# Adding the upsampled rows inside the local products, with P divided before its transposes

## Chip, cores and metric

One core of a Trainium2 chip runs the whole kernel. The metric is device time in microseconds of one execution; a kernel's time is the median over its runs. A profile of one execution gives the trace from which the rows below are taken. Engines: PE multiplies matrices, DVE and ScalarE (ACT) work on elements and read PE's results, GpSimd (POOL) works on elements in SBUF, SyncE (SP) issues most of the DMAs.

## The reference

Attention over 8 batches, 8 heads, 576 positions, 64 dimensions, in two branches that are added, and then a mixture of 8 experts. All is float32. Cut to what is computed:

```python
# coarse branch: means over 4 positions, full attention over 144, every row used for 4 positions
q_d = q.reshape(B, H, Sd, 4, D).mean(axis=3)           # k_d, v_d alike
out_up = np.repeat(softmax_attention(q_d, k_d, v_d), 4, axis=2)
# local branch: only |i - j| < 4
scores = np.where(mask, scale * q @ k.T, -1e9)
attn = np.exp(scores - max)
attn = attn / (np.sum(attn, axis=-1, keepdims=True) + 1e-09)
x = out_up + attn @ v                                  # then to (4608, 512)
# experts: logits x @ w_gate; pairs (token, expert) in falling order of logit, 576 tokens
# for each expert; out[tokens of e] = relu(x @ w1[e]) @ w2[e]
```

## The kernel before

The program has three stages: the attention with the logits, the routing, and the experts. Instructions of the attention stand on each engine exactly in the order in which the code is called; that order comes from tables of numbers.

**Local branch.** It goes in 36 units of 128 tokens. A unit u has four windows of 32 queries; the 38 keys that a window can reach lie in a block `KW`. For each unit, in units of time after u (the table `LOC`):

- `s0`, `s1` (0.33): scores of four heads each on PE, over a mask that is added by a matmul; then on DVE a maximum (`mx`, line 444) and a subtraction into the tile `sw` (line 445). ScalarE takes the exponential in place three PE pieces later (`FL`, line 446).
- `t` (1.3): four transposes of `sw` on PE (line 454), copied by ScalarE into `pt` (line 465), so that keys lie on partitions.
- `v0`, `v1` (1.83): products of `pt` with the values, 32 matmuls of 65 columns (line 476). The values are in one of four tiles `vw`, two windows to a tile half: window c takes partitions from 64 (c mod 2) on. 48 rows are loaded for a window (`VR`) of which 38 are used; rows 48 to 63 of each half have nothing. A 65th column of ones makes PE sum P, and `norm` (lines 404, 405, 407) divides by that sum on DVE while it moves the products from PSUM into `x`.
- `up` (1.7, but not before the coarse branch of the batch is through): a DMA of the upsampled rows from `up_dram` to the tile `up`, 32 rows of 2 KB, each four times, 256 KB (line 416).
- `add` (4.5): x + up (line 484), on DVE, from unit 28 on POOL. `st` (4.6): x to DRAM (line 487).
- `lt` (5.61): transposes of x (line 494), split in two halves of 16 bits by ScalarE (line 498) and DVE (line 499). `lm` (8.07): logits (lines 509, 512, 514).

**Coarse branch.** For each batch (4.5 units) q and k are transposed (`trw`, `trt`; `TW` says from when to when, counted from the batch before), summed over 4 positions (`gsum`, mostly on POOL), and then `down` runs six pieces of scores and transposes and two of products (`DW`, counted from the batch's first unit). Its last step divides on DVE, writes to `up_dram` (lines 387, 394), and `load_up` reads it back. `evac` sends the copies of transposes out of PSUM to DVE or ScalarE in turn, by the tuple `EV`: a 1 is DVE.

`run` gives every step a time, sorts them, and calls them; a PE step counts as a piece, and `after(n, f)` calls f n pieces later. `need(key)` calls it at once. All loads and stores of the attention are issued by SP in that order. `load_vw(u)` stands 1.75 units before unit u (`VWT`). The profile's lines are those of the code here:

## Time and profile before

| | us |
|---|---|
| median of 3 runs (781.58 to 786.01) | 782.59 |
| the profiled execution | 783.71 |
| its span, first to last instruction | 781.8 |
| busy in the span: PE / DVE / ACT / POOL | 681.8 / 560.7 / 332.0 / 244.0 |
| last logits of the attention reduced | 291.3 |

A row of a busy-time view gives a stretch and how long each engine worked in it. A row of waits names who waited, what ended the wait, and the total. A row of groups gives the line in the code, engine, operation, what it writes and reads, then count, busy time and mean duration, and idle time of the engine ahead of it. Idle time of an engine costs only where somebody waits for that engine.

### The profile page before, as it was taken

How to read it: one execution, taken by the hardware profiler on the slowest of the kernel's cores; microseconds unless marked ns; L12 is line 12 of the kernel's file. 1: busy time of each engine (PE TensorE's matmuls, PEld its weight loads, DVE VectorE, ACT ScalarE, POOL GpSimd, SP SyncE). 2: the span in 40 equal slices, each digit the busy share in tenths (PEclk: the TensorE clock that was granted, in tenths of full speed). 3: DMA queues.
4: the chain of work that ended last, by engine and by line, in shares of the span. 5: the costliest groups of instructions: out<-in, count | busy, mean ns of one | idle time of the engine just before them, and what ended most of it. 6: DMA issues, size and time to landing. Idle time of an engine off the chain costs nothing.

```text
span 781.8 us, 21171 instructions
## 1 busy us (share of the span) xinstructions
PE 681.8 (87%) x8565; PEld 470.8 (60%) x8565; DVE 560.7 (72%) x1679; ACT 332.0 (42%) x631; POOL 244.0 (31%) x274
## 2 busy tenths in 40 slices
PE   6788889888888863499899999999989999999994
PEld 4676778777767652365465465366457476574752
DVE  7978888778868887787969979798959645171210
ACT  3546758465576440441524425134225234262210
POOL 9455364535626340300710512121230402201001
PEclk9889999989999995599899999999999999999998
DMA  9959899897988650712615565562743783804001
GB/s 265 208 163 266 213 228 258 231 245 236 239 224 197 173 175 1 238 40 87 217 35 191 153 154 178 102 240 60 228 169 105 124 278 76 215 2 101 22 27 34
DMA packets 148133, 125.00 MB, mean 160 GB/s; under 512 B 92228, under 2 KB 122436, under 8 KB 148036
## 3 DMA queue, kind: packets, MB, share of 16 engines
q1 hardware_dynamic: 140656, 102.12, 48.6%
q0 software_dynamic: 6432, 20.98, 8.9%
q8 instruction: 68, 1.11, 0.6%
q10 hardware_dynamic: 948, 0.55, 0.3%
q14 instruction: 29, 0.24, 0.1%
HBM read 95.30 MB, written 21.23 MB: 149 GB/s over the span
## 4 chain that ended last, share of the span: by engine, by line
PE 30%; issue 25%; DVE 24%; DMA 10%; POOL 4%; ACT 4%; SPq 1%; POOLq 0%; ACTq 0%; DVEq 0%
PE pX L1135 7%; PE pH L1106 7%; POOL out_dram L1144 2%; DVE cmp L703 2%; PE pR L733 2%; DMA up<-up_dram 2%; DMA nat<-in_moe_w_dram 2%; PE g L476 2%; DVE x L407 2%; PE g L292 1%; DMA vw<-in_v_dram 1%; PE g L373 1%; DVE x L484 1%; DVE wl L1054 1%; PE g L436 1%
## 5 line engine op out<-in xcount | busy, mean ns | idle before, releaser
L1106 PE MATMUL pH<-xt,wh 128*128 128x256 f16 (+1 forms) x1024 | 196.9, 287 | 2.8 <-DMA xt<-xs 1.1
L1135 PE MATMUL pX<-wh,ht 128*128 128x512 f16 (+1 forms) x640 | 183.3, 386 | 1.9 <-DVE xt L1082 1.9
L1106 PE MATMUL pH<-xt,wl 128*128 128x320 f16 (+1 forms) x512 | 146.3, 287 | 0.0
L1135 PEld LDWEIGHTS <-ht 128*128 128x128 f16 (+1 forms) x960 | 82.5, 101 | 90.6 <-issue 7.0
L1144 POOL DMA_INDIRECT out_dram<-y,idx x40 | 44.3, 1109 | 285.2 <-ACT y L1141 226.4
L1135 PE MATMUL pX<-wl,ht 128*128 128x512 f16 (+1 forms) x320 | 119.9, 387 | 0.0
L1106 PEld LDWEIGHTS <-wh 128*128 128x128 f16 x1024 | 97.6, 98 | 29.0 <-issue 3.5
L1119 ACT ACTIVATE ht<-pH 128x512 f16<-128x512 f32 (+1 forms) x128 | 45.5, 407 | 124.1 <-PE pH L1106 124.1
L1054 DVE SCALAR_TENSOR_TENSOR wl<-nat,wh 128x512 f16<-128x512 f32 x128 | 84.8, 684 | 2.9 <-ACT wh L1052 0.7
L1069 POOL DMA_INDIRECT xg<-x_dram,idx x40 | 49.2, 1231 | 106.9 <-DVE idx L1004 36.0
L1141 ACT ACTIVATE y<-pX 128x512 f32<-128x512 f32 (+1 forms) x40 | 23.7, 593 | 131.8 <-PE pX L1135 75.9
L1122 DVE SCALAR_TENSOR_TENSOR ht<-pH,ht 128x512 f16<-128x512 f32 (+1 forms) x128 | 52.6, 452 | 34.6 <-ACT ht L1119 34.1
L1052 ACT ACTIVATE wh<-nat 128x1024 f16<-128x1024 f32 x64 | 66.8, 1055 | 10.4 <-DMA nat<-in_moe_w_dram 10.3
L1106 PEld LDWEIGHTS <-wl 128*128 128x128 f16 x512 | 50.1, 98 | 11.9
L465 ACT COPY pt<-g 64x512 f32<-64x512 f32 x72 | 41.7, 580 | 28.8 <-PE g L454 26.3
L476 PE MATMUL g<-vw,pt 128*64 128x65 f32 x1152 | 44.6, 231 | 6.7 <-ACT pt L465 4.6
L1143 DVE SCALAR_TENSOR_TENSOR y<-pX,y 64x512 f32<-64x512 f32 x8 | 5.5, 694 | 61.7 <-ACT y L1141 61.6
L476 PEld LDWEIGHTS g<-vw,pt 128*64 128x64 f32 x1152 | 39.6, 144 | 12.9 <-ACT pt L465 7.5
L292 PE MATMUL g<-ident,nat 128*128 128x128 f32 x256 | 41.9, 292 | 4.4 <-DMA nat<-in_k_dram 3.2
L265 POOL TENSOR_TENSOR gtmp<-qz 64x576 f32<-64x576 f32 x28 | 32.0, 1144 | 32.9 <-DVE kdt L268 31.2
L278 ACT COPY kt<-g 64x512 f32<-64x512 f32 (+1 forms) x56 | 35.2, 628 | 16.7 <-PE g L292 10.5
L484 DVE TENSOR_TENSOR x<-x,up 128x512 f32<-128x512 f32 x28 | 29.6, 1058 | 15.0 <-DMA up<-up_dram 15.0
(219 smaller groups left out, 1197.8 us busy)
## 6 DMA issues: line engine op xcount, KB each, us to landing
nat<-in_moe_w_dram SPq DMA_DIRECT2D x28, 1024.0 KB
vw<-in_v_dram SPq DMA_DIRECT2D x136, 96.0 KB
up<-up_dram SPq DMA_DIRECT2D x36, 256.0 KB
x_dram<-x SPq DMA_DIRECT2D x36, 256.0 KB
nat<-in_q_dram SPq DMA_DIRECT2D x16, 512.0 KB
nat<-in_k_dram SPq DMA_DIRECT2D x16, 512.0 KB
nat<-in_v_dram SPq DMA_DIRECT2D x14, 512.0 KB
up_dram<-xu SPq DMA_DIRECT2D x16, 128.0 KB
```

The lines of the kernel that those rows point to most:

```text
L292: nc.tensor.transpose(p[:, a, :, fp], src[:, 4 * hh + 2 * a + s, 2 * fp:2 * fp + 2].rearrange("p f d -> p (f d)"), self.ident)
L465: self.nc.scalar.copy(out, in_)
L476: nc.tensor.matmul(o[64 * i:64 * i + 64, 65 * h:65 * h + 65], pt[:, 2 * g + i, h].rearrange("p b q -> p (b q)"), self.vw[u % 4][:, i, 4 * ...
L484: (nc.gpsimd if u >= ADDU else nc.vector).tensor_tensor(x, x, self.up[u], op=OP.add)
L1052: nc.scalar.activation(hi, r, AF.Copy, scale=sc)
L1054: nc.vector.scalar_tensor_tensor(lo[:, a:a + LOP], r[:, a:a + LOP], sc, hi[:, a:a + LOP], op0=OP.mult, op1=OP.subtract)
L1069: self.fetched = nc.gpsimd.indirect_dma_start(out=xg[:n], out_offset=None, in_=self.x, in_offset=bass.IndirectOffsetOnAxis(ap=idx[:n, c:c ...
L1106: mm = nc.tensor.matmul(p[:, s, :s1 - s0], w[d][a][:, 128 * f:128 * f + 128], xt[:, b, d, s0:s1], start=j == 0, stop=j == len(seq) - 1)
L1119: last = nc.scalar.activation(hi, q, AF.Relu)
L1122: nc.vector.scalar_tensor_tensor(lo, q, 0.0, hi, op0=OP.max, op1=OP.subtract)
L1135: mm = nc.tensor.matmul(p[o:o + m], ht[:, f, h0:h0 + m], w[4 + f // 2][b][:, 512 * (f % 2):512 * (f % 2) + 512], start=j < parts, stop=j > ...
L1144: i = nc.gpsimd.indirect_dma_start(out=self.out, in_=y[:n], in_offset=None, out_offset=bass.IndirectOffsetOnAxis(ap=idx[:n, c:c + 1], axis=0))
```

## The change

P is divided by its sum right after the exponential, on DVE (`norm` in `loc_s`), so the column of ones goes, and ScalarE copies the products into x as they are. The upsampled rows of a unit (8 for each window, 32 in all) are loaded into partitions 48 to 55 and 112 to 119 of the unit's `vw` tile, two DMAs of 32 KB. Columns 48 to 55 of `sw` hold fixed ones, which give each query its row; the transposes carry them into `pt`, and so the products add the upsampled row. The adds are gone for all units but the first three (`OLD`), which keep the way of before. The write to `up_dram` is issued `FU` pieces after the coarse division. The coarse branch stands earlier, every second evacuation goes to DVE, there are three `sw` tiles instead of two, and the later steps of a unit have new times.

```diff
-DW = (0.15, 1.9)
-DWS = {0: (1.96, 3.4), 7: (0.82, 2.25)}
-LOC = {'up': 1.7, 'st': 4.6, 't': 1.3, 'lm': 8.07, 's0': 0.33, 's1': 0.331, 'lt': 5.61, 'v0': 1.83, 'v1': 1.831, 'add': 4.5}
+FM = 2
+FX = 1
+FU = 3
+TW = (0.16, 1.95)
+DW = ((-1.95, -0.05), (-1.4, 0.45))
+DWS = {0: (1.96, 3.4), 1: (-0.8, 0.7)}
+UPL = 0.4
+LOC = {'up': 1.2, 'st': 3.3, 't': 1.87, 'lm': 5.2, 's0': 0.33, 's1': 0.331, 'lt': 3.7, 'v0': 2.35, 'v1': 2.351}
+OLD = 3
-NSW = 2
+NSW = 3
-EV = (0,0,0,1)
+EV = (0,1)
-VWT = 1.75
+VWT = 1.6
...
             for t in self.sw:
                 nc.gpsimd.memset(t[:, :, KW:], 0.0)
+            for t in self.sw:
+                nc.gpsimd.tensor_copy(t[:, :, VR:VR + 8], self.spare[:, None].to_broadcast([128, H, 8]))
...
         def end():
             r = self.norm(o, x[:, :4], 4 + g, 4.0)
...
+            self.after(FU, put, ("u", b, g))
+
+        def put():
+            up = self.up_dram[b * G:b * G + 128, 256 * g:256 * g + 256]
+            nc.sync.dma_start(up, x[:, :4].rearrange("p h d -> p (h d)"))
...
         for b in {4 * u // NW, (4 * u + 3) // NW}:
             for g in range(2):
                 self.need(("v", b, g))
+                self.need(("u", b, g))
+        src = self.up_dram[32 * u:32 * u + 32]
+        if u >= OLD:
+            for i in range(2):
+                p0 = 64 * i + VR
+                self.nc.sync.dma_start(self.vw[u % 4][p0:p0 + 8].rearrange("p c h d -> p c (h d)"),
+                                       bass.AP(tensor=src.tensor, offset=src.offset + 8 * i * HD,
+                                               ap=[[HD, 8], [16 * HD, 2], [1, HD]]))
+            return
...
-        self.after(FL, lambda: nc.scalar.activation(t[:, :, :KW], t[:, :, :KW], AF.Exp, scale=0.125), ("l", u))
+        t = t[:, :, :KW]
+        self.after(FL, lambda: nc.scalar.activation(t, t, AF.Exp, scale=0.125), ("e", u))
+
+        def norm():
+            self.need(("e", u))
+            r = self.wk.tile([128, H], F32, name="dl", bufs=3)
+            nc.vector.tensor_reduce(r, t, axis=AX.X, op=OP.add)
+            nc.vector.tensor_scalar(r, r, 1e-9, None, op0=OP.add)
+            nc.vector.reciprocal(r, r)
+            nc.vector.tensor_tensor(t, t, r[:, :, None].to_broadcast([128, H, KW]), op=OP.mult)
+
+        self.after(FL + FM, norm, ("l", u))
...
-        self.norm(o, x[:, 256 * g:256 * g + 256].rearrange("p (h d) -> p h d", h=4), 4, 1.0)
+        if g:
+            x = self.x[u] = self.wk.tile([128, HD], F32, name="x", bufs=XB)
+            self.after(FX, lambda: nc.scalar.copy(x, o), ("o", u))
```

**How the order moves.** First DVE, at unit 24, from its maximum on (names: `den` is the reciprocal of the column of ones, `dl` that of the new sum, `xt` the halves of the transposed x, `lg` the logits, `sd` the coarse scores). Before:

```order
L444 TENSOR_REDUCE mx<-g 128x8
L445 TENSOR_TENSOR sw_131<-g,mx 128x8x38
L484 TENSOR_TENSOR x<-x,up 128x512
L499 SCALAR_TENSOR_TENSOR xt<-g,xt 128x512
L404 TENSOR_SCALAR den<-g 128x4
L405 RECIPROCAL den<-den 128x4
L407 TENSOR_TENSOR x<-g,den 128x256
L404 TENSOR_SCALAR den<-g 128x4
L405 RECIPROCAL den<-den 128x4
L407 TENSOR_TENSOR x<-g,den 128x256
L514 TENSOR_REDUCE lg<-g 128x8
```

And now, from the same maximum:

```order
L464 TENSOR_REDUCE mx<-g 128x8
L465 TENSOR_TENSOR sw_131<-g,mx 128x8x38
L472 TENSOR_REDUCE dl<-sw_131 128x8
L473 TENSOR_SCALAR dl<-dl 128x8
L474 RECIPROCAL dl<-dl 128x8
L475 TENSOR_TENSOR sw_131<-sw_131,dl 128x8x38
L534 SCALAR_TENSOR_TENSOR xt<-g,xt 128x512
L338 TENSOR_REDUCE mxd<-g 128x3
L340 TENSOR_TENSOR sd<-g,mxd 128x432
L549 TENSOR_REDUCE lg<-g 128x8
```

The add and two divisions of products out of PSUM are gone, and one division of P stands right behind the subtraction, ahead of the halves of x.

Second SP, where batch 4's coarse result goes out (`up_dram<-xu`) and the first unit that uses it, 18, reads it back. Before:

```order
L387 DMA up_dram<-xu 128x256
L487 DMA x_dram<-x 128x512
L200 DMA natt<-in_q_dram 64x1x256 x2
L200 DMA natt<-in_k_dram 64x1x256 x2
L387 DMA up_dram<-xu 128x256
L394 DMA up_dram<-xu 8x16x64
L416 DMA up<-up_dram 128x1x512
L229 DMA vw_129<-in_v_dram 48x8x64
```

And now, where unit 17's rows are loaded between the two writes:

```order
L404 DMA up_dram<-xu 128x256
L431 DMA vw_128<-up_dram 8x2x512 x2
L521 DMA x_dram<-x 128x512
L404 DMA up_dram<-xu 128x256
L406 DMA up_dram<-xu 8x16x64
L236 DMA vw_127<-in_v_dram 48x8x64 x4
L431 DMA vw_129<-up_dram 8x2x512 x2
```

The load stood right behind the write; now a unit's values stand between them, and the rows go into a `vw` tile.

Third PE, at the transposes of P (`sw`): unit 20's before, ahead of the scores of unit 21 (`kt,qz`), the logit transposes (`ident,x`) and unit 20's products (`vw,pt`):

```order
L454 MATMUL g<-ident,sw_131 128x128 x4
L428 LDWEIGHTS identb
L428 MATMUL g<-mask,identb 128x304
L436 MATMUL g<-kt,qz_119 32x38 x32
L494 MATMUL g<-ident,x 128x128 x4
L476 MATMUL g<-vw_127,pt_133 64x65 x16
```

And unit 19's now:

```order
L448 LDWEIGHTS identb
L448 MATMUL g<-mask,identb 128x304
L456 MATMUL g<-kt,qz_119 32x38 x32
L506 MATMUL g<-vw_129,pt_134 64x64 x16
L332 MATMUL g<-kdt,qdz_124 128x144 x3
L529 MATMUL g<-ident,x 128x128 x4
L332 MATMUL g<-kdt,qdz_124 128x144 x3
L485 MATMUL g<-ident,sw_132 128x128 x4
L332 MATMUL g<-kdt,qdz_124 128x144 x2
L335 MATMUL g<-kdt,qdt_125 32x144 x4
```

The transposes stood ahead of the next unit's scores; now they stand behind them, behind the products of unit 18 and pieces of batch 5's coarse scores (`kdt,qdz`).

More of the change, by code (lines that the diff above doesn't have):

```diff
@@ L106, in __init__ @@
         self.ident, ident = ident
-        identh = cst.tile([128, 130 + H], BF, name="identb")
-        self.identb, self.half, self.own8 = identh[:, :128], identh[:, 128:130], identh[:, 130:]
+        identh = cst.tile([128, 138 + H], BF, name="identb")
+        self.identb, self.half, self.own8 = identh[:, :128], identh[:, 128:130], identh[:, 130:130 + H]
+        self.spare = identh[:, 130 + H:]
         self.wm = cst.tile([128, 128], BF, name="wm")
@@ L126, in __init__ @@
         for i in range(4):
-            self.vw.append(cst.tile([128, 2, H, D + 1], F32, name=f"vw{i}"))
+            self.vw.append(cst.tile([128, 2, H, D], F32, name=f"vw{i}"))
         for i in range(NSW):
@@ L469, in loc_v @@
         if g == 0:
[L470 to L472 removed]
+            self.ov = self.ps.tile([128, 512], F32, name="g", bufs=8)
+        o = self.ov
         pt = self.ptw[u % NPT]
@@ L483, in log_a @@
         x = self.x[u]
-        (nc.gpsimd if u >= ADDU else nc.vector).tensor_tensor(x, x, self.up[u], op=OP.add)
+        self.need(("o", u))
+        nc.vector.tensor_tensor(x, x, self.up[u], op=OP.add)
     def store(self, u):
-        getattr(self.nc, STQ).dma_start(self.x_dram[128 * u:128 * u + 128], self.x[u])
+        self.need(("o", u))
+        self.nc.sync.dma_start(self.x_dram[128 * u:128 * u + 128], self.x[u])
     def log_t(self, u):
@@ L491, in log_t @@
         x = self.x[u]
+        self.need(("o", u))
         p = self.ps.tile([128, 4, 128], F32, name="g", bufs=8)
@@ L591, in run @@
                 work.append((u - VWT, 0, 0, lambda u=u: self.load_vw(u), False))
-            for j, (name, lag) in enumerate(LOC.items()):
+            for j, (name, lag) in enumerate((LOC if u >= OLD else LOC0).items()):
                 at = u + lag
-                if lag >= 2.0:
+                if lag >= 2.5:
                     at += max(E0 - u * E1, 0.0) - max(u - UE, 0) * CE * int(lag - 1)
                 if name == "up":
-                    at = max(at, end[(4 * u + 3) // NW])
+                    at = max(at, end[(4 * u + 3) // NW] + UPL)
                 work.append((at, 2, j, stage[name](u), name in PEL))
```

32 lines of the change are left out of this document (13 added, 19 removed).

## Prediction

> **What bounds the kernel now.** I read first the busy times by stage, cutting the span where the last logits are reduced (291.3 us), where the first expert's matmuls are running (340 us), and the attention into pieces of 60 us. Columns: stretch, its length, then busy time (and instructions) of each engine, granted clock, share of the DMA engines, GB/s.
>
> ```profile
> core 0: us, PE busy (x) PEld busy (x) DVE busy (x) ACT busy (x) POOL busy (x), PEclk, DMA share, GB/s
> 40.00:100.00 60.00, 51.77 (x1112) 44.90 (x1108) 47.35 (x131) 38.52 (x78) 28.51 (x37) 0.94 0.84 216
> 100.00:160.00 60.00, 51.30 (x1186) 43.41 (x1184) 51.87 (x134) 38.33 (x75) 31.26 (x41) 0.97 0.92 241
> 160.00:220.00 60.00, 53.23 (x1131) 46.17 (x1131) 48.67 (x127) 35.63 (x71) 32.95 (x42) 0.89 0.89 225
> 220.00:280.00 60.00, 50.37 (x1226) 42.68 (x1225) 50.17 (x144) 35.56 (x72) 25.47 (x34) 0.97 0.81 207
> 280.00:291.30 11.30, 6.45 (x117) 5.65 (x114) 8.57 (x27) 4.44 (x8) 3.81 (x3) 0.92 0.52 175
> 291.30:340.00 48.70, 23.64 (x233) 17.83 (x233) 38.15 (x140) 13.11 (x22) 7.43 (x7) 0.60 0.35 115
> 340.00:781.80 441.80, 416.11 (x3173) 248.85 (x3171) 283.23 (x921) 148.24 (x277) 87.80 (x75) 0.98 0.42 124
> ```
>
> The diff touches the attention alone, and on every engine the instructions from the routing on stand in the same order in both programs. So the 48.7 us of routing and the 441.8 us of experts stay; 291.3 us can move. From 40 to 280 us no engine is saturated and four are near it: PE is busy 51.77 + 51.30 + 53.23 + 50.37 = 206.7 of 240 us, so it idles 33.3; DVE is busy 198.1; the DMA engines 81 to 92%. The time goes to engines waiting for each other in turn, and the waits from 40 to 291 us say for what (total us, times, longest):
>
> ```profile
> PE g L454 <- ACT sw L446: 11.9, 9, 2.7
> PE g L355 <- ACT sd L339: 7.6, 10, 1.7
> PE g L476 <- ACT pt L465: 4.6, 6, 1.4
> DVE x L484 <- DMA up<-up_dram: 15.0, 8, 3.6
> DVE den L404 <- PE g L476: 6.4, 7, 1.7
> SPq L416 <- DMA up_dram<-xu: 14.4, 8, 3.1
> SPq L487 <- POOL x L484: 7.2, 5, 1.7
> ```
>
> PE's largest wait is line 454, the transposes of P, for the exponential of the same unit; then line 355, the transposes of the coarse P. DVE stands 15.0 us before its adds of line 484, for upsampled rows that have not landed, and everything behind them in its queue waits too. SP waits 14.4 us before loading those rows, until they are written. The chain of waits over the same 251 us (its shares by line, and two of its longest pieces) agrees:
>
> ```profile
> by line: issue 6.1%; DMA up<-up_dram 6.0%; DVE x L407 4.7%; PE g L476 4.5%; PE g L292 4.2%; DMA vw<-in_v_dram 4.0%; PE g L373 4.0%; DVE x L484 4.0%; PE g L436 3.9%; DMA nat<-in_v_dram 3.1%; PE g L454 2.9%; DVE xt L499 2.7%; PE g L325 2.7%;
> 147.30 3.12 DMA up<-up_dram
> 223.19 5.11 DMA up<-up_dram
> ```
>
> The landing of `up` is 6.0% = 15.1 us of the chain, line 407 4.7% = 11.8, line 484 4.0% = 10.0. All three are taken away or replaced. But a chain does not say what becomes the longest path next; PE's 33.3 us of idling is the ceiling of any gain before 280 us, since its work is the same but for one column in 65 of line 476, which I count as nothing.
>
> **DVE, part by part.** Groups (count | busy us, mean ns | idle before), the copy of `qz` from the view that keeps shapes apart:
>
> ```profile
> L407 DVE TENSOR_TENSOR x<-g,den 128x256 f32<-128x256 f32 x70 | 29.7, 425 | 2.4
> L484 DVE TENSOR_TENSOR x<-x,up 128x512 f32<-128x512 f32 x28 | 29.6, 1058 | 15.0 <-DMA up<-up_dram 15.0
> L405 DVE RECIPROCAL den<-den 128x4 f32<-128x4 f32 (+1 forms) x86 | 15.4, 179 | 3.0
> L404 DVE TENSOR_SCALAR den<-g 128x4 f32<-128x4 f32 (+1 forms) x86 | 13.2, 153 | 7.8 <-PE g L476 6.4 <-PE g L382 1.3
> L445 DVE TENSOR_TENSOR sw<-g,mx 128x304 f32<-128x304 f32 x33 | 15.7, 475 | 1.1
> L444 DVE TENSOR_REDUCE mx<-g 128x8 f32<-128x304 f32 x33 | 15.5, 468 | 4.5 <-PE g L436 4.3
> L276 DVE COPY qz<-g 64x512 f32<-64x512 f32 x24 | 16.5, 689 | 3.3 <-PE g L292 2.7 <-ACT qz L278 0.2
> L498 ACT ACTIVATE xt<-g 128x512 f16<-128x512 f32 x36 | 21.5, 597 | 8.7 <-PE g L494 8.1
> L446 ACT ACTIVATE sw<-sw 128x304 f32<-128x304 f32 x34 | 15.6, 458 | 26.6 <-DVE sw L445 26.6
> ```
>
> Gone: after each unit's products two times line 404, 405 and 407, 72 x (153 + 179 + 425) ns = -54.5 us; 25 of the 28 adds on DVE (three units keep theirs), 25 x 1058 ns = -26.5. The eight adds on POOL go too.
>
> New, 36 times: sum over P, plus 1e-9, reciprocal, multiply. The sum is priced by line 444, a reduction of the same 304 elements, 0.47; the two short ones by lines 404 and 405, 0.15 + 0.18. The multiply reads two SBUF operands, of which these rows tell (minimum, median, maximum in ns):
>
> ```profile
> L484 DVE TENSOR_TENSOR x<-x,up x28: 679/1020/1709, 60.4 to 255.4; 128x512 f32<-128x512 f32 x28
> L268 DVE TENSOR_TENSOR kdt<-gtmp x9: 457/459/1407, 17.9 to 245.4; 128x288 f32<-128x288 f32 x9
> L265 POOL TENSOR_TENSOR gtmp<-qz x28: 1137/1143/1188, 34.8 to 248.5; 64x576 f32<-64x576 f32 x28
> L428 PE MATMUL g<-mask,identb x36: 289/292/461, 13.6 to 277.1; 128*128 128x304 bf16 x36
> ```
>
> Line 268 on DVE, 288 elements, has 0.46 as median but 1.41 at worst; line 484, 512 elements, 0.68 at best, 1.02 median, 1.71 at worst. 304/512 of the median gives 0.61; bounds 0.46 and 1.41. Each unit costs 0.47 + 0.15 + 0.18 + 0.61 = 1.41 (1.26 to 2.21), so +50.8 us (45 to 80). In the Trainium skill, "SBUF — State Buffer", section "SBUF: two separate sides", DVE instructions with two SBUF inputs and GpSimd instructions share one port pair as a lock held for a whole instruction. The spread of line 484 agrees, since its excess of 1.03 us is about one POOL instruction of 1.14 us. By that rule, with POOL busy 49% of the time (118 of 240 us) and half an instruction to wait on average, an estimate of the multiply is 0.46 + 0.28 = 0.74, and the sum on DVE would be some 5 us worse than mine.
>
> EV sends every second evacuation to DVE instead of every fourth: by the order of the instructions 24 more copies of 64x512, at 689 ns = 16.5, and 12 smaller ones at 0.4 to 0.69, say 0.6 = 7.2; together +23.7.
>
> DVE's sum: -54.5 - 26.5 + 50.8 + 23.7 = -6.5 us, from -12 to +23. Its waits: the 15.0 for `up` go. A new one comes: in 13 of the 33 later units nothing stands on DVE between the subtraction (line 445) and the new sum, which needs ScalarE's exponential (0.46, line 446), so DVE stands about 0.55 us there, with everything behind it: +7. The den wait (6.4 us behind line 476) goes over to ScalarE, which has the room. In all DVE gets about 14 us, and is no longer what PE stands for most.
>
> **ScalarE.** 36 copies of 128x512 out of PSUM at 597 ns (line 498 has the shape) are +21.5; 36 evacuations fewer, by the same row 24 x 0.60 + 12 x 0.5 = -20. Even, and it is busy 148 of 240 us.
>
> **PE.** Between a unit's scores and its transposes stood the logit transposes, the products before and the logits; now the next unit's scores, products and often pieces of the coarse attention stand between as well, since `t` goes from 1.3 to 1.87 units. The chain to cover grows from subtract and exp by the four new instructions, 1.41 plus two handoffs, 1.7 us; the lag grows by 0.57 units. Line 428 starts once for each unit, 36 times from 13.6 to 277.1, so a unit is 7.5 us, and the lag brings 4.3. Of the 11.9 us I take 8 (0 to 11.9). The coarse attention of a batch moves from on top of the next batch's transposes to between two sets of them; units were heavy and light, and the waits sit in the light ones. I take 3 us (0 to 8) of the other waits, 7.6 and 4.6, for this. Transpose to product goes from 0.53 to 0.48 units: nothing. POOL's group sums have less time to the coarse scores, but POOL is busy half the time.
>
> **The new wait: products need the upsampled rows.** The reader moves from the add, 2.8 units behind the load, to the products, 1.15 units behind it: 1.15 x 7.5 = 8.6 us. Landings took 3.12 and 5.11 us, so SP may be 3.5 to 5.5 us late. It is later now. The load of unit 19 (20th issue of line 416) stands at 20.7 units in the program, between the scores of units 20 and 21 at 20.33 and 21.33:
>
> ```profile
> 173.47 0.29 PE L428 MATMUL g<-mask,identb 128*128 128x304 bf16 x1 [0.28 <-ACT qz L278]
> 178.02 0.29 PE L428 MATMUL g<-mask,identb 128*128 128x304 bf16 x1
> 188.16 0.69 SPq L416 DMA_DIRECT2D up<-up_dram  x1
> ```
>
> It was issued 10 us after the later and 15 after the earlier. If that lag stayed, every product would wait. What speaks against it: 14.4 us of SP's lag are the waits for `up_dram`, whose write used to be issued with the load right behind it and now stands most of a unit ahead; 7.2 us are for POOL's adds, which go; the load carries 64 KB instead of 256; and once PE has waited, SP has caught up. Against that there is one issue more for each unit (0.69 us at most, by the row above), and the `vw` load now stands right behind the products that free its tile, so that SP waits there if it is early. I take +2 us of PE waiting, between 0 and the 15 us that the adds lose now.
>
> **The end of the attention.** The last unit, in order of time:
>
> ```profile
> 278.16 0.47 DVE L444 TENSOR_REDUCE mx<-g 128x8 f32<-128x304 f32 x1
> 279.24 0.45 ACT L446 ACTIVATE sw<-sw 128x304 f32<-128x304 f32 x1
> 279.97 0.63 PE L454 MATMUL g<-ident,sw 128*128 128x128 f32 x4
> 281.93 1.22 PE L476 MATMUL g<-vw,pt 128*64 128x65 f32 x32 [0.89 <-ACT pt L465]
> 285.67 1.26 POOL L484 TENSOR_TENSOR x<-x,up 128x512 f32<-128x512 f32 x1 [0.81 <-DMA x_dram<-x]
> 289.06 0.25 PE L512 MATMUL g<-wg,xt 128*128 128x8 f16 x4 [0.47 <-DVE xt L499]
> ```
>
> From the exp to the logits stand t, copies, products (281.93 to 283.15), norm, POOL's add, which ends at 286.93, and the last transposes to 289.31. After: exp ends at 279.69, P's division 1.41 and handoffs (1.6), t and the copies (279.97 to 281.93) 2.0, products 1.2, copy 0.6, then the same 2.4 as from 286.93 to 289.31: 287.5. I take -2 us. The last coarse attention stands 1.8 units earlier, so its rows are there.
>
> **The beginning.** Four more small fills on POOL and the coarse attention of batch 1 moved 0.95 units up into a stretch where the DMA engines are the limit: +1 (0 to 4).
>
> **Sum.** -8 - 3 + 2 - 2 + 1 = -10 us. The profiled execution took 783.7 us (span 781.8 and 1.9 around it), 1.1 over the median of 782.6. 773.7 against it is 772.6 against the median; I say 772.5. From no change to one measured, 0.5% or 3.9 us is about what counts.
>
> **Rivals.**
> (1) A larger gain, under 766 us: the rows of the chain that are removed were its longest links (15.1 + 11.8 + 10.0), and PE's idling halves: -17 and -2 at the end, 764. Against it: in order, DVE and ScalarE still hand P back and forth, with one handoff more. 0.14.
> (2) Nothing, 778.7 to 786.5: the division costs DVE its upper bound, 80 us instead of 50.8, and DVE, 198 of 240 busy, remains the one that PE follows. DVE gains nothing, the 11.9 us wait of line 454 remains with another cause (the multiply instead of the exp), and only the end's 2 us are left: 781. The median of line 484 far over its minimum speaks for it, the 0.46 median of line 268 against. 0.20.
> (3) Slower: SP's lag stays, and PE itself stands for the upsampled rows. Deciding point: SP more than 5.5 us behind PE at the load. With all of the adds' 15 us on PE, and only the end's 2 us and 5 of the transposes' gained: 783.7 + 15 - 7 = 791.7, or 790.6 of the median. The lag shown above speaks for it, that it comes mostly from waits that go speaks against. 0.14.
> The forecast, 766 to 778.7, has 0.52.
>
> The range reaches from a little over halving PE's idling to the lower part of rival 3: 762 to 786; the likeliest case alone 766 to 778.7. Faster by over 0.5%: 0.52 + 0.14 = 0.66; within: 0.20; slower: 0.14.
>
> **What would show it.** In the profile after: the last logits near 281 us instead of 291.3; PE's wait of the P transposes (now for DVE's multiply) under 4 us; waits of the products for `up_dram` rows about 2 us, and over 10 would be rival 3; the multiply about 0.6 us, over 1.0 would be rival 2; SP's waits for `up_dram` near nothing; routing and experts within 1 us of 490. The forecast is wrong if PE's busy share from 40 us to the end of the attention does not rise from 86% to about 89%.

## The result, and the profile after

The changed kernel takes 805.46 us as the median of 4 runs (802.23 to 806.93), beside 783.84 (781.58 to 786.01) for the kernel before on the same chip: ratio 1.025, 95% interval 1.021 to 1.030. It is slower; the prediction said 772.5. The profiled execution took 805.63 us, its span 803.9. In the sets of runs of the experiments the kernel before took 776 to 783 us, so they are compared by their ratio to it. The last logits are reduced at 309.2 us instead of 291.3: 17.9 us of the loss lie in the attention, 4.2 behind it.

Busy time by stage, after (columns as before; the next to last row is the routing with the first 9 us of the experts, the last row the rest):

```profile
core 0: us, PE busy (x) PEld busy (x) DVE busy (x) ACT busy (x) POOL busy (x), PEclk, DMA share, GB/s
40.00:100.00 60.00, 46.15 (x900) 40.13 (x899) 49.08 (x115) 30.86 (x67) 28.94 (x38) 0.91 0.75 212
100.00:160.00 60.00, 48.82 (x1048) 43.90 (x1047) 48.02 (x108) 34.89 (x66) 25.75 (x36) 0.91 0.68 190
160.00:220.00 60.00, 50.79 (x1141) 44.90 (x1141) 47.56 (x111) 35.72 (x72) 23.19 (x30) 0.93 0.69 191
220.00:280.00 60.00, 49.66 (x1095) 43.64 (x1096) 50.39 (x117) 34.42 (x70) 32.43 (x49) 0.94 0.60 164
280.00:309.20 29.20, 21.53 (x643) 19.19 (x630) 19.55 (x54) 17.27 (x33) 0.00 (x0) 1.00 0.43 124
309.20:358.00 48.80, 19.25 (x189) 14.65 (x189) 33.31 (x130) 10.62 (x19) 11.77 (x7) 0.55 0.35 114
358.00:803.90 445.90, 421.12 (x3217) 252.58 (x3215) 287.90 (x931) 150.70 (x281) 82.58 (x75) 0.99 0.41 123
```

PE is busy 195.4 of 240 us from 40 to 280, not 206.7: 81%, where 89% was forecast. No engine became fuller; DVE has 195.0, the DMA engines went from 81 to 92% down to 60 to 75%. So nothing is saturated, and the loss is waiting: up to the last logits PE's own work, the same 5161 instructions, took 243.2 us instead of 242.1 (at a granted clock of 0.92 instead of 0.94 from 40 to 280 us), 1.1 of the 17.9 us. The waits from 40 us to the last logits:

```profile
PE g L506 <- ACT pt L496: 24.3, 16, 3.6
PE g L332 <- POOL qdz L275: 8.4, 7, 2.0
PE g L362 <- ACT sd L346: 6.2, 9, 1.1
ACT sw L467 <- DVE sw L465: 58.5, 31, 5.2
DVE dl L472 <- ACT sw L467: 7.9, 15, 0.5
SPq L236 <- PE g L506: 43.1, 17, 5.3
```

What was to go has gone: the transposes of P waited 11.9 us for the exponential, now 3.5 us for the multiply (the row of line 485 below), and the products have no wait for upsampled rows among these. Two others took the place: the products (line 506) wait 24.3 us for the copies of P, 4.6 before, and the coarse scores (line 332) wait 8.4 us for POOL's sums over 4 positions (`qdz`), for which the kernel before did not wait at all. Groups up to the last logits, and the multiply by itself (minimum, median, maximum in ns):

```profile
L475 DVE TENSOR_TENSOR sw<-sw,dl 128x304 f32<-128x304 f32 x36 | 22.5, 626 | 1.2
L485 PE MATMUL g<-ident,sw 128*128 128x128 f32 x144 | 22.5, 280 | 3.5 <-DVE sw L475 3.5
L472 DVE TENSOR_REDUCE dl<-sw 128x8 f32<-128x304 f32 x36 | 16.7, 464 | 8.1 <-ACT sw L467 7.9
L473 DVE TENSOR_SCALAR dl<-dl 128x8 f32<-128x8 f32 x36 | 11.5, 320 | 1.2
L474 DVE RECIPROCAL dl<-dl 128x8 f32<-128x8 f32 x36 | 7.3, 203 | 1.2
```

```profile
L475 DVE TENSOR_TENSOR sw<-sw,dl x36: 475/476/1450, 29.6 to 297.9; 128x304 f32<-128x304 f32 x36
```

By part of the attention, from the start of a unit's scores in the two traces (4th and 32nd run of the mask's matmul, line 428 before, 448 after): unit 3 starts at 52.1 us instead of 48.4 (+3.7); from there to unit 31 it takes 227.2 us instead of 203.4, 8.11 us a unit instead of 7.26 (+23.8); from there to the last logits 30.0 instead of 39.5 (-9.5). These three numbers, called beginning, pace and end, are given below for the experiments too.

Behind the attention, the 4.2 us lie ahead of the experts, in the first load of gathered rows of x, which POOL issues. The pairs are of before and of after; the second line of each is the first expert's first product:

```profile
319.24 1.51 POOL L1069 DMA_INDIRECT xg<-x_dram,idx  x1 [32.31 <-DMA nat<-in_moe_w_dram]
326.83 0.58 PE L1106 MATMUL pH<-xt,wh 128*128 128x256 f16 x2 [0.68 <-DMA xg<-x_dram,idx]
337.03 6.39 POOL L1104 DMA_INDIRECT xg<-x_dram,idx  x1 [57.53 <-DMA nat<-in_moe_w_dram]
349.19 0.59 PE L1141 MATMUL pH<-xt,wh 128*128 128x256 f16 x2 [0.68 <-ACT xt L1116]
```

The load is issued as long after the last logits as before (27.8 us, 27.9), but it takes 6.39 us instead of 1.51. The experts start 40.0 us after the last logits instead of 35.5, and from there to the end it is 454.7 us, 455.0 before.

### The profile page after: what moved, and what is told of

Read it like the earlier page. It is cut to its first block, busy times and chain, and to the rows that moved or that the text cites. A ratio compares the mean times of both kernels' runs of the same rounds, so it can differ in the third digit from the quotient of the medians.

```text
span 803.9 us, 21117 instructions
## 1 busy us (share of the span) xinstructions
PE 683.6 (85%) x8565; PEld 478.2 (59%) x8565; DVE 567.6 (71%) x1618; ACT 329.6 (41%) x631; POOL 230.4 (29%) x270
## 3 DMA queue, kind: packets, MB, share of 16 engines
q1 hardware_dynamic: 137488, 95.63, 42.1%
## 4 chain that ended last, share of the span: by engine, by line
PE 32%; issue 25%; DVE 23%; ACT 7%; DMA 6%; POOL 4%; SPq 1%; POOLq 0%; ACTq 0%; DVEq 0%
PE pX L1170 7%; PE pH L1141 7%; PE g L506 4%; POOL out_dram L1179 2%; PE pR L768 2%; DVE cmp L738 2%; PE g L332 2%; DMA nat<-in_moe_w_dram 2%; DVE kt L283 2%; ACT kt L285 2%; PE g L380 2%; ACT pt L496 1%; DVE qz L283 1%; PE g L299 1%; DVE wl L1089 1%
## 5 line engine op out<-in xcount | busy, mean ns | idle before, releaser
L1176 ACT ACTIVATE y<-pX 128x512 f32<-128x512 f32 (+1 forms) x40 | 23.7, 594 | 131.5 <-PE pX L1170 75.7
L1157 DVE SCALAR_TENSOR_TENSOR ht<-pH,ht 128x512 f16<-128x512 f32 (+1 forms) x128 | 52.5, 451 | 34.7 <-ACT ht L1154 34.2
L506 PE MATMUL g<-vw,pt 128*64 128x64 f32 x1152 | 48.4, 243 | 26.7 <-ACT pt L496 24.3
L506 PEld LDWEIGHTS g<-vw,pt 128*64 128x64 f32 x1152 | 43.4, 155 | 30.1 <-ACT pt L496 28.4
L299 PE MATMUL g<-ident,nat 128*128 128x128 f32 x256 | 39.6, 292 | 8.1 <-DMA nat<-in_q_dram 4.5
L467 ACT ACTIVATE sw<-sw 128x304 f32<-128x304 f32 x36 | 16.5, 459 | 64.0 <-DVE sw L465 64.0
L272 POOL TENSOR_TENSOR gtmp<-kt 128x576 f32<-128x576 f32 x7 | 8.6, 1235 | 114.2 <-ACT kt L285 67.2
L299 PEld LDWEIGHTS g<-ident,nat 128*128 128x128 f32 x256 | 31.0, 151 | 11.1 <-issue 7.3
```

The source lines that it names most:

```text
L299: nc.tensor.transpose(p[:, a, :, fp], src[:, 4 * hh + 2 * a + s, 2 * fp:2 * fp + 2].rearrange("p f d -> p (f d)"), self.ident)
L506: nc.tensor.matmul(o[64 * i:64 * i + 64, D * (4 * g + h):D * (4 * g + h) + D], pt[:, 2 * g + i, h].rearrange("p b q -> p (b q)"), self.vw[ ...
L1157: nc.vector.scalar_tensor_tensor(lo, q, 0.0, hi, op0=OP.max, op1=OP.subtract)
```

## The experiments

| kernel | ratio to before (95%) | unit 3 at, us | pace, us a unit | end, us |
|---|---|---|---|---|
| before | 1 | 48.4 | 7.26 | 39.5 |
| after | 1.025 (1.021 to 1.030) | 52.1 | 8.11 | 30.0 |
| evacuations of before | 1.021 (1.017 to 1.025) | 53.5 | 7.82 | 30.7 |
| exponential later | 1.040 (1.036 to 1.044) | 57.4 | 8.25 | 32.2 |
| coarse attention later | 1.026 (1.022 to 1.030) | 51.8 | 7.88 | 34.3 |
| t earlier | 1.036 (1.030 to 1.042) | 53.4 | 8.03 | 31.5 |
| adds kept | 1.042 (1.038 to 1.046) | 53.5 | 8.31 | 36.3 |
| division alone, old times | 1.046 (1.041 to 1.051) | 50.4 | 8.03 | 48.2 |
| old instructions, new times | 1.018 (1.015 to 1.022) | 46.4 | 7.95 | 33.0 |
| no division | 1.017 (1.013 to 1.021) | 49.0 | 7.89 | 29.5 |
| products later | 1.019 (1.012 to 1.026) | 52.9 | 7.71 | 35.5 |
| the same, evacuations of before | 1.019 (1.013 to 1.025) | 52.1 | 7.60 | 35.6 |
| old, lags of t and products | 0.996 (0.992 to 0.999) | 49.0 | 7.15 | 42.1 |
| old, coarse place and transposes | 1.025 (1.019 to 1.031) | 49.4 | 8.27 | 29.7 |
| old, coarse place | 1.018 (1.012 to 1.025) | 48.4 | 8.08 | 29.7 |
| old, coarse place, sums behind | 1.002 (1.000 to 1.004) | 47.4 | 7.70 | 31.1 |
| after, sums behind | 1.039 (1.033 to 1.046) | 51.9 | 8.31 | 37.2 |
| after, sums behind, no division | 1.037 (1.032 to 1.041) | 50.2 | 7.93 | 37.9 |
| after, old coarse place | 1.024 (1.019 to 1.030) | 52.5 | 7.40 | 44.5 |
| after, all with room | 1.014 (1.009 to 1.018) | 52.7 | 7.05 | 44.8 |

The three columns behind the ratio are of one profiled execution each. Those of the experiments come from other sets of runs than the first two rows, so a difference of a few us between two rows says little.

**First: one suspected wait at a time.** Three guesses at one cause: DVE overloaded, ScalarE's order, the group sums.

```diff
-EV = (0,1)
+EV = (0,0,0,1)
```

> The change with EV back at (0,0,0,1): a quarter of the evacuations on DVE, as before, instead of half. Theory 'DVE load': the 24 us of copies that were moved to DVE make its subtraction late, the exponential on ScalarE stands for it (58.5 us of waits), and the copies of the transposed P behind it come late for the products. Then at least half of the 22 us comes back: 790 to 795 us, and ScalarE's wait for the subtraction falls from 58.5 to under 40. Theory 'ScalarE order': ScalarE gets 22 us more to do ahead of the same late copies, so nothing comes back or it gets worse: 804 to 812, products' wait for the copies 24 us or more.

```diff
-FL = 3
+FL = 8
```

> The change with the exponential 8 pieces behind the scores instead of 3 (and the division of P 10 instead of 5), so that on ScalarE it no longer stands as far ahead of the copies of the unit before. Theory 'ScalarE order': the exponential's wait for DVE no longer holds the copies up; the products' wait for them falls from 24 us to under 12 and the time to 790 to 797. Theory 'DVE load': the wait only changes its place, 802 to 808.

```diff
-DW = ((-1.95, -0.05), (-1.4, 0.45))
+DW = ((-1.15, 0.75), (-1.05, 0.8))
```

> The change with the coarse attention 0.8 (even batches) and 0.35 units (odd) later, which its readers still allow. Theory 'group sums': PE's 8.4 us of waits for POOL's sums before the coarse scores go, and as they hold the whole queue 6 to 9 us come back: 796 to 800. Both other theories: they are covered by the other waits, 803 to 808.

```diff
-LOC = {..., 't': 1.87, ...}
+LOC = {..., 't': 1.45, ...}
```

> The change with the transposes of P at 1.45 units instead of 1.87, so 0.90 units ahead of the products instead of 0.48. Theory 'ScalarE order' (too little room between transposes and products for ScalarE's queue): products' wait for the copies under 8 us, against a few us of PE's wait for the division of P that come back; 787 to 795. Theory 'DVE load': PE then waits for the division instead, by as much; 802 to 808.

None brought the loss back. The times expected above are beside the 784 us of the first set; in this set the kernel before took 777, so the 792 and 796 us that were measured look like hits and are not: only the ratios count. With the evacuations of before, DVE was busy 178 instead of 195 us of the 240, and the ratio fell by 0.4%, within the intervals. ScalarE's wait for the subtraction fell from 58.5 to 43.1 us, PE's for the copies of P rose to 29.8, and the result lies between the two theories: DVE's load is at most a small part of the loss. The others each cut the wait that they aimed at and lost it elsewhere. The exponential later: copies of P 18.4 us instead of 24.3, but 11.4 for the multiply. The coarse attention later: no wait for the sums, but 7.3 for upsampled rows. t earlier: copies of P 13.2, but 18.8 for the sums. Where each single cure fails, either the theory of one cause is wrong or the places are tied together; so next the parts of the change were separated.

**Second: instructions against timetable.** Two kernels with the old and the new times crossed, and two that take one half of the new instructions out.

The kernel after with all of its tables (`LOC0`, `TW`, `DW`, `DWS`, `EV`, `VWT`, and also `NEXT`, `XB`, `UPL`) as before, adds kept. It has two `sw` tiles again, and all 36 adds stand on DVE, where the kernel before has the last eight on POOL:

```diff
-OLD = 3
+OLD = 36
-LOC0 = {..., 't': 1.87, ..., 'v0': 2.35, ...}
+LOC0 = {..., 't': 1.3, ..., 'v0': 1.83, ...}
```

> The kernel before with one part of the change: P is divided before its transposes and ScalarE copies the products out; the upsampled rows stay a 256 KB tile and an add, and every time in the table, the evacuations' turns and the values' loads are those of before. Theory 'division' (one more hand-over from ScalarE to DVE and back to PE in each unit's chain, 50 us more work on DVE with 54 us less behind the products): ratio 1.015 to 1.03, last logits 303 to 310 us, PE waiting over 15 us for the multiply at the transposes of P, since t stands only one piece behind the next division. Theory 'timetable' (the loss is in the new order of the pieces): 0.99 to 1.005, last logits 288 to 294. Theory 'rows in the tiles' (SP's loads bound to the products): 0.99 to 1.005 too.

The kernel before with the tables of after (`'t': 1.87`, `'v0': 2.35`, `'lm': 7.2`, `TW`, `DW`, `DWS`, `EV`, `VWT`, `NEXT`):

> The kernel before with its own instructions (division behind the products, 256 KB tile of upsampled rows, adds) but with the changed kernel's timetable: coarse attention 1.5 to 2.1 units ahead, the fine transposes of the next batch squeezed into 1.79 units, t at 1.87, products at 2.35, every second evacuation on DVE, values' load 1.6 units ahead. Theory 'timetable': ratio 1.015 to 1.03, last logits 303 to 310 us, PE waiting 15 to 25 us for the copies of P at the products and 5 to 10 for group sums at the coarse scores. Theory 'division' or 'rows in the tiles': 0.985 to 1.005, last logits at most 294, these waits under 8 and 3.

The kernel after with the adds kept:

```diff
-OLD = 3
+OLD = 36
```

> The changed kernel with one part undone: upsampled rows come as a 256 KB tile and are added on DVE as before (36 adds, some 30 us more on DVE); P is still divided ahead, and the timetable is the new one. Theory 'timetable': ratio 1.02 to 1.04 (the loss stays, and the adds come on top). Theory 'division': 1.02 to 1.04 as well. Theory 'rows in the tiles': 0.99 to 1.01, as SP has nothing left that stands behind the products but the values' load of three units on.

The kernel after without lines 472 to 475:

```diff
         def norm():
             self.need(("e", u))
-            r = self.wk.tile([128, H], F32, name="dl", bufs=3)
-            nc.vector.tensor_reduce(r, t, axis=AX.X, op=OP.add)
-            nc.vector.tensor_scalar(r, r, 1e-9, None, op0=OP.add)
-            nc.vector.reciprocal(r, r)
-            nc.vector.tensor_tensor(t, t, r[:, :, None].to_broadcast([128, H, KW]), op=OP.mult)
```

> The changed kernel without its four new instructions on DVE in each unit (sum, plus 1e-9, reciprocal, multiply): the local attention is left undivided, so the routing gets other numbers and only the attention's part of the time, up to the last logits, is compared. DVE has 51 us less to do. Theory 'division': last logits back to 288 to 294 us (from 309), PE's wait for the copies of P under 8. Theory 'timetable': 302 to 310, PE's waits for the copies of P and for group sums stay at 20 and more together. Theory 'rows in the tiles': 302 to 310 too, SP's wait of 40 us behind the products stays.

The old instructions lose 1.8% from the new times alone, and show the same two waits at about the same size, 24.3 and 8.4 us in the changed kernel (PE's waits up to the last logits):

```profile
PE g L476 <- ACT pt L465: 24.2, 17, 3.0
PE g L325 <- POOL qdz L268: 10.7, 7, 2.5
```

So those waits belong to the timetable, not to the division. The division has its own price: with the old times, where t comes one piece behind it, the kernel with it is 4.6% slower, more than was expected, and PE waits at the transposes of P for the multiply and, behind it, for a reduction of logits on DVE (its two largest waits):

```profile
PE g L485 <- DVE sw L475: 25.5, 12, 5.8
PE g L485 <- DVE lg L549: 15.8, 3, 6.5
```

With the new times the steps are: old instructions 1.018, with the division (adds kept) 1.042, with the rows in the tiles besides 1.025. In this timetable the division costs about 2.4%, and the rows in the tiles give about 1.7% back. The first step holds also what goes with the division: ScalarE's copy of the products, the last eight adds on DVE instead of POOL, and the later write of the coarse rows (`FU`, `UPL`). Leaving the division out of the changed kernel leaves 1.017 (its routing then works on other numbers); the last logits come at 299.4 us instead of 309.2, between what the theories 'division' and 'timetable' expect, and its waits for the copies of P stay at 24.4 us, as 'timetable' has it.

**Third: which part of the timetable.** In the kernel before, one part each.

```diff
-LOC = {..., 't': 1.3, ..., 'v0': 1.83, 'v1': 1.831, ...}
+LOC = {..., 't': 1.87, ..., 'v0': 2.35, 'v1': 2.351, ...}
-VWT = 1.75
+VWT = 1.6
...
-                if lag >= 2.0:
+                if lag >= 2.5:
```

> The kernel before with only the lags of the fine steps changed: t at 1.87 instead of 1.3, products at 2.35 instead of 1.83, values' load 1.6 units ahead. Coarse attention, transposes and evacuations as before. If the closeness of t and products costs by itself: PE's wait for the copies of P rises from 4 to over 15 us, the wait for the exponential goes, ratio 1.01 to 1.02. If it is the coarse attention's place that does it: ratio 0.99 to 1.003.

```diff
-TW = (0.23, 2.44)
+TW = (0.16, 1.95)
-DW = (0.15, 1.9)
+DW = ((-1.95, -0.05), (-1.4, 0.45))
-DWS = {0: (1.96, 3.4), 7: (0.82, 2.25)}
+DWS = {0: (1.96, 3.4), 1: (-0.8, 0.7)}
```

> The kernel before with only the coarse attention 1.5 to 2.1 units ahead and the next batch's transposes within 1.79 instead of 2.21 units. t and products at 1.3 and 1.83 as before, evacuations as before. If the coarse attention's place costs by itself: PE waits 6 to 12 us for group sums, ratio 1.01 to 1.02. If it is t and the products: ratio 0.99 to 1.003, and the wait for upsampled rows on DVE (15 us) goes down.

The lags alone: 0.996 (0.992 to 0.999), the fastest kernel of this study and, by this interval, a little faster than before. Its trace does not show where: the last logits come at 291.5 us, beside 291.3 in the trace of the kernel before, from another set. The wait of the transposes for the exponential (11.9) goes, that of the products for the copies of P rises:

```profile
PE g L476 <- ACT pt L465: 14.4, 7, 3.4
```

The coarse attention's place and the squeezed transposes alone: 1.025, as much as the whole change, and more than the 1.01 to 1.02 expected. Here one wait stands out, and the trace shows how it comes about. First the waits of this kernel, then PE and POOL in order of time around batch 3's last transposes (line 292) and coarse scores (line 325):

```profile
PE g L325 <- POOL qdz L268: 14.7, 9, 2.0
PE g L476 <- ACT pt L465: 3.2, 4, 0.9
```

```profile
110.68 0.66 PE L292 MATMUL g<-ident,nat 128*128 128x128 f32 x4 [0.20 <-ACT kt L278]
113.98 1.00 PE L325 MATMUL g<-kdt,qdz 128*128 128x144 f32 x6
116.83 0.51 PE L325 MATMUL g<-kdt,qdz 128*128 128x144 f32 x2 [1.16 <-POOL qdz L268]
119.27 0.85 PE L325 MATMUL g<-kdt,qdz 128*128 128x144 f32 x2 [1.93 <-POOL qdz L268]
```

```profile
106.89 1.15 POOL L265 TENSOR_TENSOR gtmp<-kt 128x576 f32<-128x576 f32 x1 [20.96 <-ACT kt L278]
114.95 1.14 POOL L265 TENSOR_TENSOR gtmp<-qz 64x576 f32<-64x576 f32 x1 [1.46 <-DVE den L404]
116.17 0.60 POOL L268 TENSOR_TENSOR qdz<-gtmp 64x256 f32<-64x256 f32 x1
117.05 1.14 POOL L265 TENSOR_TENSOR gtmp<-qz 64x576 f32<-64x576 f32 x1
118.27 0.94 POOL L268 TENSOR_TENSOR qdz<-gtmp 64x256 f32<-64x256 f32 x1
```

POOL idles 20.96 us, and then works on one batch's sums from 106.89 to past 119 us. PE comes to the coarse scores at 113.98, 2.6 us after the last transposes end (110.68 + 0.66), and is held at 116.83 and at 119.27. In the kernel before it comes to batch 3's scores 11.3 us after the last transposes (103.87 to 115.15), and line 325 waited for three things, and POOL is not among them:

```profile
  ACT qz L278: 3.0, 4
  DVE x L407: 0.6, 2
  ACT pt L465: 0.5, 2
```

**Fourth: is it that wait, and only that?** The coarse place alone, without the squeezing; the same work with nothing that waits for the sums; and the latter in the changed kernel.

In the kernel before:

```diff
-DW = (0.15, 1.9)
-DWS = {0: (1.96, 3.4), 7: (0.82, 2.25)}
+DW = ((-1.95, -0.05), (-1.4, 0.45))
+DWS = {0: (1.96, 3.4), 1: (-0.8, 0.7)}
```

> The kernel before with the coarse attention 1.5 to 2.1 units ahead and nothing else (the transposes keep their 2.21 units, so the group sums have still less time: 0.1 to 0.6 units). Theory 'coarse place': ratio 1.02 to 1.045, PE's wait for group sums 15 us or more. If it was the squeezing of the transposes in the run with both: ratio under 1.01.

On top of the coarse place and the squeezed transposes:

```diff
                         if b and s and w == "k":
-                            self.gsum(b, "k", 2 * hh)
-                            self.gsum(b, "q", 2 * hh)
+                            if b < 2:
+                                self.gsum(b, "k", 2 * hh)
+                                self.gsum(b, "q", 2 * hh)
...
+        def last(f=fs[-1]):
+            f()
+            for a in (0, 2):
+                self.gsum(b, "k", a)
+                self.gsum(b, "q", a)
```

> The kernel before with new coarse place and squeezed transposes (ratio 1.025 when it was run), but from batch 2 on the group sums of q and k are made behind the batch's coarse attention, which reads the sums of two batches earlier: the same instructions, other data, and nothing that the coarse scores wait for. If the wait for the group sums is the cause: the 14.7 us at line 325 go to under 2, ratio 0.995 to 1.008, last logits 290 to 297. If it is the bunching of PE's work or of the DMA loads: ratio stays over 1.015.

> The changed kernel with the same edit: group sums of q and k from batch 2 on behind the coarse attention, which reads older sums. If the wait for the sums is the cause there too: ratio 1.0 to 1.01 (from 1.025), last logits 290 to 299. If it is only its share of the waits (8.4 us of some 40): ratio 1.013 to 1.02. If the waits move on: over 1.02, with the copies of P waited for over 25 us.

The coarse place alone gives 1.018, so the squeezing is at most a small part. With the sums behind, the same instructions take 1.002 (1.000 to 1.004). POOL is no longer among the waits of line 325, of which the longest is now the second row here (the first is PE's largest wait):

```profile
PE g L476 <- ACT pt L465: 6.8, 8, 1.5
PE g L325 <- DVE mxd L331: 1.8, 1, 1.8
```

So in the old instructions this wait makes the new place a loss: shown by taking it away with the work kept. It is not all that the new place costs. Of the 28.0 us that units 3 to 31 had lost (231.4 us instead of 203.4), 15.7 came back; of the 12.3 that remain an end that is 8.5 us shorter and a beginning that is 1.1 us shorter make up most. In the changed kernel the same edit made it slower, 1.039: the coarse scores no longer wait for sums, but PE waits 28.5 us for copies of P and 7.0 once for DVE. That is what was expected for "if the waits move on". DVE's wait for the coarse scores themselves rose from 5.2 to 12.8 us there; that this is the reason is not shown.

**Fifth: the changed instructions with room.** Products and coarse attention later; the coarse attention where it was; both costs out; and room everywhere.

```diff
-DW = ((-1.95, -0.05), (-1.4, 0.45))
+DW = ((-1.15, 0.75), (-1.05, 0.8))
-LOC = {..., 'st': 3.3, 'lm': 5.2, 'lt': 3.7, 'v0': 2.35, 'v1': 2.351}
+LOC = {..., 'st': 3.7, 'lm': 5.6, 'lt': 4.1, 'v0': 2.75, 'v1': 2.751}
-VWT = 1.6
+VWT = 1.2
```

> The changed kernel with more room in its timetable: products (and all behind them) 0.4 units later, at 2.75, with t at 1.87 as it is; coarse attention 0.8 and 0.35 units later, so that the group sums have 1.9 and 1.0 units before it and the upsampled rows still 1.6 to 2.0 units behind it; values' load 1.2 units ahead. Theory 'room' (the new timetable gives three hand-overs too little room at once: copies of P, group sums, upsampled rows; easing one alone only starves another): PE's waits for the copies of P under 8 us and for the group sums under 3, none for upsampled rows over 3, ratio 0.99 to 1.005, last logits 285 to 295 us. Theory 'queues' (DVE and ScalarE are so entangled that the waits move on to other lines whatever the lags): ratio 1.015 to 1.03, last logits 303 and more, the 25 us of waits turn up elsewhere.

And with `EV = (0,0,0,1)` besides:

> The same with every fourth evacuation on DVE instead of every second. Theory 'room': within 0.5% of the one before, to either side. Theory 'queues': DVE's 17 us less shorten what others wait for, ratio 0.5 to 1% lower than the one before.

```diff
-DW = ((-1.95, -0.05), (-1.4, 0.45))
+DW = ((0.15, 1.9), (0.15, 1.9))
-TW = (0.16, 1.95)
+TW = (0.23, 2.44)
-LOC = {..., 'st': 3.3, 't': 1.87, 'lm': 5.2, 'lt': 3.7, 'v0': 2.35, 'v1': 2.351}
+LOC = {..., 'st': 4.5, 't': 1.87, 'lm': 6.4, 'lt': 4.9, 'v0': 3.6, 'v1': 3.601}
```

with `EV`, `DWS` and `NEXT` as before and `VWT = 0.35`:

> The changed kernel's instructions (division of P ahead, rows in the values' tiles) with the coarse attention and the transposes where they were before (0.15 to 1.9 and 0.23 to 2.44 units); so that the rows are there in time, the products stand 1.25 units later, at 3.6, and what is behind them too; every fourth evacuation on DVE, values' load 0.35 units ahead. Theory 'coarse place' (the loss comes from the coarse attention being close behind its own batch's transposes and group sums): PE waits under 3 us for group sums and under 6 for copies of P, ratio 0.985 to 1.0, last logits 280 to 291 us. Theory 'division' (the longer chain costs as well): ratio 1.01 to 1.02, PE waits over 10 us for the copies of P or for the multiply.

Sums behind and lines 472 to 475 left out, the two edits shown above together:

> The changed kernel with both suspected costs taken out: the group sums from batch 2 on stand behind the coarse attention (as in the run that came out at 1.039), and the four instructions of the division are left out (as in the run that came out at 1.017), so the local attention is undivided and the coarse attention reads older sums. If these two are the whole loss: last logits at 290 us or earlier against about 291 of the kernel before, ratio under 1.003. If the short way from t to products, which both earlier runs kept (24 to 26 us of waiting for copies of P), costs by itself: ratio 1.01 to 1.02, that wait again over 18 us.

From the kernel with the old coarse place: `'t': 2.6`, `'v0': 4.3`, what is behind them 0.7 later, `VWT = -0.35`, `FU = 1` instead of 3:

> The changed kernel's instructions with the transposes and the coarse attention where they were before, and all hand-overs given room: t at 2.6 (division), products at 4.3 (copies of P; upsampled rows 2 units behind their batch instead of 1.3), the rows written two pieces earlier, every fourth evacuation on DVE. If lack of room is the whole loss, and the changed instructions gain by themselves: no wait of PE over 4 us but those inside the coarse attention, pace of a unit 7.0 us or less (7.26 before), ratio 0.985 to 0.998. If the division costs whatever its room (ScalarE and DVE wait for each other once more in every unit): ratio 1.008 to 1.02, pace 7.3 to 7.5 and the end of the attention (from the scores of unit 31 to the last logits) 42 to 46 us instead of 39.5.

The pace falls step by step as room is given: 8.11, then 7.71 and 7.60 with later products, 7.40 with the old coarse place, 7.05 with all. The ratios do not follow: 1.019 twice, 1.024 and 1.014, where the theory of missing room expected at most 1.005, 1.0 and 0.998. In the last, PE's waits for the copies of P and for the sums are no longer among the larger ones:

```profile
PE g L362 <- ACT sd L346: 13.3, 10, 1.8
PE g L506 <- DMA vw<-up_dram: 6.9, 4, 4.3
```

That pace, below the 7.26 of before, is the only place where the changed instructions gained, (7.26 - 7.05) x 28 = 5.9 us. They lose it at both ends: unit 3 starts 4.3 us later and the end is 5.3 us longer, so this kernel is still slower, 1.014. Its profile is of the fastest of its runs, 784.1 us against a median of 791.3; the 7.1 us between them are more than the gain, so that the pace of its other runs is below 7.26 is not shown. The kernel with both suspected costs out (sums behind, no division) stayed at 1.037, over both expectations, with 32.7 us of waiting for copies of P. It does not say what the two cost: putting the sums behind makes the changed kernel slower by itself, with the division (1.025 to 1.039) and without (1.017 to 1.037).

## Why the prediction was wrong

The prediction counted the waits that the change takes away, and put at nothing, or at a gain, what the new order brings. By the steps of the second group of runs, the new times were to gain 11 us (8 and 3 of PE's waits) and cost the old instructions 1.8%, some 14 us. The division's hand-over was to be paid by the longer lag and cost 2.4%, some 18 us. The upsampled rows were to cost 2 us and gave 1.7% back, some 13 us. The steps are differences of ratios that are each known to about 0.4%. The signs that the prediction had named for the old waits came true (3.5 us at the transposes of P, none for upsampled rows, a multiply of 0.63 us); it had named none for the two new ones.

- **The coarse attention's move: the step that failed.** The prediction booked it as a gain ("I take 3 us (0 to 8) of the other waits") and dismissed what spoke against it: "POOL's group sums have less time to the coarse scores, but POOL is busy half the time". A mean over the stage says nothing about a burst that has a deadline. POOL's sums of a batch come in one burst behind its transposes; by `TW` and `DW` the coarse scores used to come 1.7 units behind the transposes (odd batches) or 2.7 (even), and now come 0.65 and 1.1 behind. Measured in the old instructions: 1.8 to 2.5%, 14 to 19 us lost instead of 3 gained. In the changed kernel its share is not known: with the coarse attention back in its old place and the products later the ratio was still 1.024.
- **"Transpose to product goes from 0.53 to 0.48 units: nothing".** Wrong: the wait went from 4.6 to 24.3 us. What counts is not the distance but what ScalarE does in it. ScalarE and PE of the changed kernel at unit 18, whose transposes are done at 185.56:

```profile
184.84 0.46 ACT L467 ACTIVATE sw<-sw 128x304 f32<-128x304 f32 x1 [1.60 <-DVE sw L465]
185.32 0.59 ACT L511 COPY x<-g 128x512 f32<-128x512 f32 x1
185.80 1.30 ACT L285 COPY kt<-g 64x512 f32<-64x512 f32 x2
187.11 0.60 ACT L533 ACTIVATE xt<-g 128x512 f16<-128x512 f32 x1
187.72 1.24 ACT L285 COPY kt<-g 64x512 f32<-64x512 f32 x2
188.99 1.18 ACT L496 COPY pt<-g 64x512 f32<-64x512 f32 x2
```

```profile
184.96 0.60 PE L485 MATMUL g<-ident,sw 128*128 128x128 f32 x4
185.82 0.79 PE L456 MATMUL g<-kt,qz 128*32 128x38 f32 x64
190.22 1.09 PE L506 MATMUL g<-vw,pt 128*64 128x64 f32 x14 [3.61 <-ACT pt L496]
```

  ScalarE works without a gap, but it waited 1.60 us for DVE's subtraction first and then has the copy of x, four evacuations and one half of a transposed x ahead of the copies of P, 3.7 us of work, so PE stands 3.61 us. ScalarE's wait for the subtraction is 58.5 us in all, 26.6 before. In the old instructions the lags alone raise the wait to 14.4 while the transposes' 11.9 go, and the ratio is 0.996: "of the 11.9 us I take 8" was right that this wait goes, and wrong that most of it is gained.
- **DVE's sum, -6.5 us.** By rows it is about nothing: all DVE rows up to the last logits add up to 260.5 us before and 260.8 after. (The busy time, which counts instructions that overlap once, went from 239.3 to 246.4.) The 36 evacuations more were right, +23.4 for +23.7. The division took 16.7 + 11.5 + 7.3 + 22.5 = 58.0 us, within the 45 to 80 given and above the 50.8 taken. The multiply was right (0.63 for 0.61); the +1e-9 was not, 0.32 us for 0.15, with a median of 0.17 and a maximum of 1.05. But rival 2, DVE as the bound, was not the cause either: without the division DVE had 154 us of 240, and the products waited as long. What the division costs is a place in the chain, which the old times show (1.046).
- **Upsampled rows, +2 us; rival 3.** The kernel came out slower, which only rival 3 had, at 0.14, but not by its mechanism: the changed kernel does not wait for these rows, and none of PE's waits from 40 us on is for the loads behind which SP waits 43.1 us. Such a wait appeared where the coarse attention came later in the program (7 to 11 us), and in the run with both costs out (7.6).
- **DVE's wait for the exponential, +7.** Measured 7.9.
- **Beginning, +1; end, -2.** The beginning measured +3.7. The chain that the -2 was for, from the last exponential to the last logits' product, did not get shorter: 10.3 us (296.88 to 307.21) instead of 9.6 (279.69 to 289.31), where 7.8 was forecast.

```profile
296.42 0.46 ACT L467 ACTIVATE sw<-sw 128x304 f32<-128x304 f32 x1 [1.31 <-DVE sw L465]
306.95 0.26 PE L547 MATMUL g<-wg,xt 128*128 128x8 f16 x4 [0.76 <-DVE xt L534]
```

  The last five units together, the end of the table, took 9.5 us less. With the coarse place alone in the old instructions the end is 29.7 too, so that gain is of the coarse attention being over earlier, which the prediction put at nothing but "its rows are there".
- **Routing and experts within 1 us of 490.** They took 494.7 us, since the first gathered load took 6.39 us instead of 1.51. That "the instructions from the routing on stand in the same order" is no reason for the same time. In the traces this load takes 1.5 us in all six kernels of the old instructions and 6.4 in eight of the fourteen of the changed ones, from 1.5 to 4.7 in the six others. No run tells why.

**What stays open.** That the new timetable leaves three hand-overs too little room at once (copies of P, group sums, upsampled rows) agrees with the pace falling as room is given. What speaks against it is that its own ratios were missed. What the changed kernel loses to each was not separated: taking away the sums' wait alone made it slower, for a reason that no run here isolates. Nor was a kernel tried that has the roomy middle with the short end of the changed kernel, 30.0 us instead of 44.8; that it would beat the kernel before is a guess.

## To carry to other kernels

When work with a deadline is moved closer to what feeds it, count the burst in between (here 12 us of sums on an engine that idled 21 us before it), not the mean load of the engine. Where engines work in order, a wait taken from one place came back here at another, so a timetable is to be tried in parts, first in the old instructions: one run of the coarse move alone would have shown the loss. And an added hand-over (ScalarE to DVE to PE) is a term of its own: it cost 4.6% with its consumer one piece behind it and about 2.4% with 0.57 units more; that it is free with still more room no run here shows.

## Not expected of the hardware

The multiply took 475 ns at best and in the median, but up to 1450; the same spread stands in the 128x8 add of line 473 (median 171, maximum 1045). The trace shows what the long ones go together with. One of the longest multiplies, and the POOL instruction that was running when it began:

```profile
222.40 1.45 DVE L475 TENSOR_TENSOR sw<-sw,dl 128x304 f32<-128x304 f32 x1
222.37 1.15 POOL L272 TENSOR_TENSOR gtmp<-qz 64x576 f32<-64x576 f32 x1
```

All twelve multiplies that took 0.71 us or more began while a POOL instruction ran, and each ended 0.33 us (within 0.01) after that one's end; the 24 others, 0.47 or 0.48 us each, began when none ran. The eleven longer adds of line 473, which read one operand, ended 0.02 to 0.04 us after such a POOL instruction. The sum of line 472, which reads one operand too, has no such spread (453 to 471 ns). The Trainium skill, "SBUF — State Buffer", section "SBUF: two separate sides", has DVE instructions with two SBUF inputs and GpSimd's share one port pair, which the multiplies here agree with; the mean of 626 lies between the 0.61 us taken from the rows and the 0.74 estimated from that page.
